# Hash products of both halves in one PSUM bank, with four small transfers, in an attention-and-MLP kernel

## The chip, the cores and the metric

The kernel runs on one core of a Trainium2 chip. The metric is device time in microseconds (us) of one execution. The median of three runs of the kernel before is 780.22 us (779.61 to 780.36).

A core has TensorE (PE, matmuls into PSUM), VectorE (DVE), ScalarE (ACT) and GpSimd (POOL); SyncE (SP) issues most transfers, ScalarE a few. Each works through its own instructions in order and waits where data isn't there.

## What is computed

Attention over 2 x 8 heads of 768 rows and 64 columns, in which a query sees only keys of the same hash bucket, then two MLPs. Cut to what matters:

```
q_bits = einsum(q, proj) > 0 ; k_bits = einsum(k, proj) > 0      # proj: 64 x 6, so six bits a row
mask   = q_bucket == k_bucket
scores = where(mask, 0.125 * q @ k.T, -1e9)
attn   = exp(scores - max) / sum ; x = attn @ v                  # per head; x becomes 1536 x 512
xn     = x / sqrt(mean(x*x) + 1e-6) * rms_g
y      = (silu(xn @ w_gate) * (xn @ w_val)) @ w_out              # 512 -> 1536 -> 512
out    = relu(y @ w_in)**2 @ w_out2                              # 512 -> 2048 -> 512
```

## The kernel before

**Tiles.** Each of 16 heads has six tiles of 128 query rows, 96 in all (`plan_slot`). For a tile TensorE makes scores S of 128x768 (`st_S`, line 626) from two sets of operands: q1 with k1 (128 rows: the value's rounded part and its rest) and q2 with k2 (76 rows). Rows 64 to 75 of q2 and k2 are the hash bits, scaled by plus or minus 2^17, so that a pair of unlike buckets gets a huge negative score: the mask comes out of the matmul itself. VectorE copies S to SBUF and takes the row's extreme value on the way (`st_min`, 637), ScalarE takes the exponential (655). Then the probabilities are split into two 16-bit parts and transposed. In tiles of kind "x" TensorE transposes (674) into one of three PSUM banks `mo`, ScalarE casts (Tx, 375) and VectorE subtracts (384). In tiles of kind "a" ScalarE casts (hla), GpSimd subtracts (384), and a transfer on SP transposes (667). Then the product with V (700) into O; after a head's last tile VectorE makes the reciprocal of the sums (708, 715) and O is scaled into `xall`, by ScalarE in six pieces (722) or by VectorE in one instruction (727).

**The hash of a head** (`hash_pe`, 494): eight matmuls of 128x384 (507) into a whole score tile S, which is 2 x 384 columns in two banks and comes from the same ring as scores. Rows 64 to 75 hold the query's bits, 96 to 107 the key's. `hash_bits` (516) thresholds rows 64 to 107, both halves at once, straight into q2; `hash_dma` (524) moves the key's rows 96 to 107 of q2 to rows 64 to 75 of k2, one transfer of 12x768. Head 0 has its own short way (532 to 545).

**The norm and the MLPs.** When a batch of eight heads is done, `plan_norm` squares xall (939, ScalarE), takes the root, scales, transposes on TensorE (982) and splits into a high part `x_hi` (990, ScalarE) and a low part `x_lo` (388, VectorE). The products (1121, 1233, 1244) use weights that are made on the way: a weight of 64-bit words is loaded, ScalarE takes an absolute value (1065), VectorE does four steps (1071, 1076, 1081, 1085), and then it is split in two (375 or 379; 384). The first batch's products run beside the second batch's attention.

**The order.** Nothing is written out by hand. `Plan` is a list scheduler that runs when the program is built: every operation has a cost for each engine that may do it, needs and buffers, and a rank; at each step the operation that can start first goes next, and ties go by rank. Ranks are constants by kind of work (`R_HASH`, `R_HDMA`, `R_X`) plus a shift per operation out of the packed table `SHIFTS`. A pair such as `D=(0.47, H_E)` is a cost and a delay that make an engine less welcome. `W0` and `W1` set how many idle matmuls (454) fill gaps at the start.

Of the kernel before, what the change touches and what calls it, by code (L numbers as in the profile page):

```python
# [12 lines left out]
F32 = mybir.dt.float32  # L13
F32R = mybir.dt.float32r
# [11 lines left out]
RQ, RK = 64, 96  # L26
NH = RK + 2 * NB
# [75 lines left out]
H_E = 2.0  # L103
# [9 lines left out]
    'c-rk(XLMFYx88eBdEb|WmIwrpA`um731A>dM>>cCQuKoa5RsyRPw666Kro;nQl+RADFGo!wNW(`gFr;86d{0+kn+CgoS'  # L113
    'E7Cp1Z#L=dSPmxa<D8e|Tn{bJm%ev(8@g?AgyVspfdh679?%v_aEx1$HKjp1~AM5G$~jS)K@{;R$@xSP5OI1|2|?7W<>'
    '0;nVn|$fWf&hHA>4@*ZTmZDqRqGxftxULn*_+pvjD!#Q3%BMy&Kf)URaXpYw7=r}EN$LJlfR1T1b#1whl+vv97-*k0dO'
    '}FCOI+=F3sro&=g$nhTd{K4LeQCFssfO#BZk|&}x4?!6a6m6s4f#{uk>1fidXrSKbd<yST!@WjMfqK%0cB8S-JJJgeZ8'
    '1(aVyBc4)hDBF=9s?jqUI?+Nd_spAe&SRCVrzuaeEPtZzjHh}JWuP)(o=XHlkF&bhiR&Zc~8G^F{n6ZnSl8$1JN@kL#q'
    'T59G3+Kjug1<b=;6c4Qef8kE=3$+z?@Oqvqt`=^=w!D?M_>s592$iR7-PSs8%`wv;B0qL&f`SS9Hd>eq)ePW7Zw}N!Ee'
    '^T!aWOv+rHyjNRX_UQ#mAH=7jR9uX$|(q(E|CDH-PFzX2J?Q$i+NJ&k`+ghxfJUCQ2AC9^<=|f}ijKC`*T=A?~S)dJyH'
    '|eqr-ncutQ~cOVzq`@D>$lQM_DqjV1ARcJ$F@K0_HzhMt9(k*l}1mQ9*lNyt$n|Mr|w|B!#IuD(&MR0;TfG=|ec|(`u>'  # L120
    'ogWWg(xvWv<)VOj=)%b0+zT)7on=r(OB)(=Z^FYb$}wL7QMq;osQ%h7w}{6GtS}V`ejaVkNEsIbW3ufI-_s6rQiXbr7w'
    'BCo6p0=H{K#PIe@F(G|`Cn&=~G4D{-7Ch1>WfouT*L7lq(tN;Q|kPU<99d+C0D{=g%=N!-F1NB4}7%%@mmJv6{`{GuL9'
# [191 lines left out]
def tile_hash_attention_moe(  # L314
# [55 lines left out]
    def f32(x):  # L370
        return x.bitcast(F32)
# [1108 lines left out]
```

## Time and profile before

| | |
|---|---|
| median of three runs | 780.22 us |
| the profiled execution | 781.11 us, its span 779.3 us |
| TensorE busy | 761.0 us, 98% of the span |
| VectorE busy | 672.7 us, 86% |
| ScalarE busy | 451.1 us, 58% |
| GpSimd busy | 230.7 us, 30% |
| mean granted TensorE clock | 0.995 |

The profile is of one execution. Busy shares are averages over stages with different limits, so the stages are read apart, from windows. The attention of the first batch fills the span up to about 139 us, the second batch's runs beside the first MLP's products up to about 304 us, and products alone follow to the end. TensorE's ends are modelled, so that a short wait can hide in its busy time. Register, semaphore and transfer-issuing instructions don't count as busy.

### The profile page before, as it was taken

To read this page: it belongs to the slowest core of one execution; us is meant where nothing else is said; L and a number is where in the kernel's file an instruction comes from. 1 tells how busy PE (TensorE), PEld (TensorE's weight loads), DVE (VectorE), ACT (ScalarE), POOL (GpSimd) and SP (SyncE) were. 2 spreads that over 40 slices of the span, in tenths; PEclk is the share of its full clock that TensorE was granted. 3 is DMA by queue.
4 is the path that set the end of the run, shared out by engine and by line. 5 is a ranking of instruction groups with operands and counts; after the bars stand their busy time and mean duration, and the time that the engine had idled before them with its cause. 6 is when DMAs were issued, how large, how long until landed. Compare 5 with 4: busy or idle time off the path is not lost.

```text
span 779.3 us, 14432 instructions
## 1 busy us (share of the span) xinstructions
PE 761.0 (98%) x5401; PEld 689.8 (89%) x5401; DVE 672.7 (86%) x1340; ACT 451.1 (58%) x898; POOL 230.7 (30%) x196
## 2 busy tenths in 40 slices
PE   8999998999999999999999999999999999999998
PEld 5788887988899999999999999988888888888886
DVE  8989899898799999999998899998579787797754
ACT  5899999868877789545543344455523243232320
POOL 6689866665676445300000000010000000000000
PEclk9999999999999999999999999999999999999999
DMA  8599875998998999423342443323111131111004
GB/s 253 129 192 184 170 161 142 162 233 191 212 176 174 190 187 202 115 108 136 135 136 81 151 147 136 118 76 131 55 55 54 55 108 54 55 55 54 28 1 162
DMA packets 127726, 100.65 MB, mean 129 GB/s; under 512 B 106548, under 2 KB 108596, under 8 KB 127656
## 3 DMA queue, kind: packets, MB, share of 16 engines
q1 hardware_dynamic: 126736, 97.34, 49.9%
q10 hardware_dynamic: 920, 2.40, 1.1%
q8 instruction: 42, 0.69, 0.4%
q14 instruction: 28, 0.23, 0.1%
HBM read 67.12 MB, written 3.15 MB: 90 GB/s over the span
## 4 chain that ended last, share of the span: by engine, by line
PE 77%; DVE 7%; ACT 6%; DMA 4%; issue 3%; POOL 2%; SPq 0%; ACTq 0%; POOLq 0%; DVEq 0%
PE mo L1121 38%; PE mo L1244 17%; PE mo L1233 12%; PE S L626 4%; PE O L700 4%; DMA Ta<-hla 3%; DVE Pa L637 1%; ACT hla L375 1%; POOL hla L384 1%; PE mo L674 1%; DVE Px L637 1%; ACT Pa L655 1%; ACT xall L722 1%; DMA wraw<-in_w 1%; ACT Px L655 1%
## 5 line engine op out<-in xcount | busy, mean ns | idle before, releaser
L1121 PE MATMUL mo<-xTA,wih 128*128 128x384 f32 (+1 forms) x512 | 138.5, 351 | 0.4 <-DVE wil L384 0.4
L1121 PE MATMUL mo<-xTD,wih 128*128 128x384 f32 (+1 forms) x512 | 136.9, 348 | 0.0
L384 POOL TENSOR_TENSOR hla<-Pa,hla 128x768 f16<-128x768 f32 x66 | 111.2, 1686 | 69.1 <-ACT hla L375 50.6
L1260 DVE TENSOR_TENSOR acc<-acc,mo 128x512 f32<-128x512 f32 (+1 forms) x164 | 100.2, 616 | 21.9 <-PE mo L1244 17.5
L1121 PEld LDWEIGHTS mo<-xTA,wih 128*128 128x128 f32 x512 | 92.9, 188 | 6.2 <-DVE wil L384 0.5
L1121 PEld LDWEIGHTS mo<-xTD,wih 128*128 128x128 f32 x512 | 93.4, 188 | 5.0
L1157 ACT ACTIVATE mt<-mo 128x512 f32<-128x512 f32 x48 | 28.7, 598 | 117.8 <-PE mo L1121 117.7
L626 PE MATMUL S<-k,q 76*128 76x384 f32 (+1 forms) x384 | 86.5, 352 | 4.5 <-DVE Pa L637 2.1
L1121 PE MATMUL mo<-xTA,wil 128*128 128x384 f32 (+1 forms) x256 | 89.4, 349 | 0.0
L1121 PE MATMUL mo<-xTD,wil 128*128 128x384 f32 (+1 forms) x256 | 89.0, 348 | 0.0
L379 POOL TENSOR_SCALAR wih<-wv 128x512 fp32r<-128x512 f32 x14 | 9.4, 668 | 265.5 <-DVE wv L1085 259.4
L626 PEld LDWEIGHTS S<-k,q 76*128 76x128 f32 (+1 forms) x384 | 64.9, 189 | 9.4 <-DVE Pa L637 4.3
L637 DVE TENSOR_SCALAR_CACHE_REDUCE Pa<-S 128x768 f32<-128x768 f32 x66 | 62.8, 952 | 7.5 <-PE S L626 7.4
L1065 ACT ACTIVATE wv<-wraw 128x512 f32<-128x512 f32 x82 | 54.5, 671 | 21.3 <-DMA wraw<-in_w 17.1
L1233 PE MATMUL mo<-yh,woh 128*128 128x384 f32 x192 | 65.3, 340 | 0.5 <-DVE wil L384 0.4
L1161 DVE TENSOR_TENSOR mu<-mt 128x512 f32<-128x512 f32 x48 | 33.3, 693 | 37.1 <-ACT mt L1157 37.0
L655 ACT ACTIVATE Pa<-Pa,b 128x768 f32<-128x768 f32 x66 | 62.2, 942 | 4.5 <-DVE b L648 1.4
L1233 PE MATMUL mo<-yh,wol 128*128 128x384 f32 x192 | 64.7, 337 | 0.0
L1233 PE MATMUL mo<-yl,woh 128*128 128x384 f32 x192 | 64.6, 337 | 0.0
L375 ACT CAST hla<-Pa 128x768 f16<-128x768 f32 x66 | 55.0, 835 | 5.5 <-DMA Ta<-hla 4.8
L1081 DVE SCALAR_TENSOR_TENSOR wv<-wraw,wv 128x512 uint32<-128x512 uint32 x82 | 56.5, 692 | 0.9
L1085 DVE SCALAR_TENSOR_TENSOR wv<-wraw,wv 128x512 uint32<-128x512 uint32 x82 | 55.7, 684 | 0.4
(152 smaller groups left out, 1815.3 us busy)
## 6 DMA issues: line engine op xcount, KB each, us to landing
wraw<-in_w SPq DMA_DIRECT2D x104, 512.0 KB, 3.8
rk<-in_k SPq DMA_DIRECT2D x12, 384.0 KB, 4.1
vr<-in_v SPq DMA_DIRECT2D x8, 384.0 KB, 4.5
out<-acc SPq DMA_DIRECT2D x12, 256.0 KB, 2.0
q<-q SPq DMA_DIRECT2D x15, 192.0 KB, 3.4
rq<-in_q SPq DMA_DIRECT2D x12, 192.0 KB, 5.0
rk<-in_k ACTq DMA_DIRECT2D x4, 384.0 KB
Ta<-hla SPq DMA_TRANSPOSE x66, 4.8
```

The lines of the kernel that those rows point to most:

```text
L375: nc.scalar.copy(out_, in_)
L384: engine[eng].tensor_tensor(out=out_, in0=in0, in1=in1, op=ALU.subtract)
L626: nc.tensor.matmul(sp[:, hf, 0:TB], d[a][0:kr, t * 128:(t + 1) * 128], d[b2][0:kr, hf * TB:(hf + 1) * TB], start=(n == 0), stop=(n == 1),)
L637: nc.vector.tensor_scalar(out=e["P"].rearrange("p (a b) -> p a b", a=2), in0=e["sp"][:, :, 0:TB], scalar1=-1e9 / SCALE, scalar2=None, op0= ...
L655: nc.scalar.activation(e["P"], e["P"], AF.Exp, bias=e["b"], scale=SCALE)
L1065: nc.scalar.activation(t, f32(wst[m]["hi"]), AF.Abs)
L1081: nc.vector.scalar_tensor_tensor(out=t, in0=hi, scalar=0xC0000000, in1=t, op0=ALU.bitwise_and, op1=ALU.bitwise_or)
L1085: nc.vector.scalar_tensor_tensor(out=t, in0=lo, scalar=29, in1=t, op0=ALU.logical_shift_right, op1=ALU.bitwise_or)
L1121: nc.tensor.matmul(ps, a[:, c * 128:(c + 1) * 128], b2[:, c, :], start=(c == 0 and n == 0), stop=(c == 3 and n == 2),)
L1233: nc.tensor.matmul(po, a[:, dc * 128:(dc + 1) * 128], b2, start=(j == 0 and n == 0), stop=(j == len(fs) - 1 and n == 2),)
L1244: nc.tensor.matmul(po, a[:, tt * 128:(tt + 1) * 128], b2, start=(j == 0 and n == 0), stop=(j == len(fs) - 1 and n == 2),)
L1260: nc.vector.tensor_tensor(out=ac, in0=ac, in1=st["p"], op=ALU.add)
```

## The change

The hash weights `wz` get 96 more columns of zeros on the left. A slice of 128 columns out of it (`hash_at`) puts the twelve bit columns at any row. The eight matmuls of a head now all add into one bank of 384 columns from the ring `mo`: the query's two halves at rows 0 and 32, the key's at 64 and 96. One threshold takes all 108 rows by 384 columns to a buffer of the ring `wv` in SBUF. Four transfers of 12x384, one a side and a half, bring the bits to q2 and k2. The scores of a head wait for all four.

Further: squares and `x_hi` of the norm may be done by VectorE as well as by ScalarE; the delay `H_E` on VectorE for the evacuation of O is 0.3, not 2.0; `SHIFTS` is a new table; `wk`, a second copy of hash weights, is gone.

```diff
-H_E = 2.0
+H_E = 0.3
 SHIFTS = (
-    'c-rk(XLMFYx88eBdEb|WmIwrpA`um731A>dM>>cCQuKoa5RsyRPw666Kro;nQl+RADFGo!wNW(`gFr;86d{0+kn+CgoS'
...
+    'c-rk(_jguBx874udsAo<n$mlaZfF;zmmsKs0sSDfP=!#1NJsz!qWIAwfk1#DT|fw2`6wa+p-Pb=f=Ou7gcOpzZ{E|U+_'
...
+    wz = ap.tile([128, 2, 2, RW + 128], F32R, name="wz")
-        nc.vector.tensor_copy(wk[:, :, RQ:RQ + 2 * NB], f32(wz[:, 1, :, RK:RK + 2 * NB]))
...
+    def hash_at(c, n, row):
+        return wz[:, c, n, RW - row:RW - row + 128]
+
     def hash_pe(eng, h):
 
         d = heads[h]
-        hp = d["hp"] = scores(s_ring(h * QT + h))
+        hp = d["hp"] = mo()[:, 0:TB]
         parts = [
-            (wz[:, 0, 0], d["q1"]), (wz[:, 0, 1], d["q1"]),
-            (wz[:, 1, 0], d["k1"]), (wz[:, 1, 1], d["k2"]),
+            (c, n, x, hf) for c, n, x in ((0, 0, "q1"), (0, 1, "q1"), (1, 0, "k1"), (1, 1, "k2"))
+            for hf in range(2)
         ]
-        for n, (a, b2) in enumerate(parts):
-            for hf in range(2):
-                nc.tensor.matmul(
-                    hp[:, hf, 0:TB], a, b2[:, hf * TB:hf * TB + TB],
-                    start=(n == 0), stop=(n == 3),
-                )
+        for j, (c, n, x, hf) in enumerate(parts):
+            nc.tensor.matmul(
+                hp, hash_at(c, n, BITS["qk"[c]][hf]), d[x][:, hf * TB:hf * TB + TB],
+                start=(j == 0), stop=(j == len(parts) - 1),
+            )
 
     def hash_bits(eng, h):
 
+        hb = heads[h]["hb"] = junk()[:, 0:TB]
         nc.vector.tensor_scalar(
-            out=heads[h]["q2"][RQ:NH, :].rearrange("p (a b) -> p a b", a=2),
-            in0=heads[h]["hp"][RQ:NH, :, 0:TB],
-            scalar1=thr[RQ:NH, 0:1], scalar2=thr[RQ:NH, 1:2], op0=ALU.is_gt, op1=ALU.mult,
-        )
-
-    def hash_dma(eng, h):
-        d = heads[h]
+            out=hb[0:NH], in0=heads[h]["hp"][0:NH], scalar1=thb[0:NH, 0:1],
+            scalar2=thb[0:NH, 1:2], op0=ALU.is_gt, op1=ALU.mult,
+        )
+
+    def hash_dma(eng, h, side, hf):
+        d, row = heads[h], BITS[side][hf]
         engine[eng].dma_start(
-            out=f32(d["k2"][RQ:RQ + 2 * NB, :]), in_=f32(d["q2"][RK:RK + 2 * NB, :])
+            out=f32(d[side + "2"][rows, hf * TB:hf * TB + TB]), in_=d["hb"][row:row + 2 * NB]
         )
...
-                r=["wz", ("ql", h, 0), ("k2", h, 0)], new=[(s_ring(h * QT + h), b)],
+                r=["wz", ("ql", h, 0), ("k2", h, 0)], new=[("mo", b)],
...
     def squares(eng, t):
-        nc.scalar.activation(junk(), xall[:, t, :], AF.Square, accum_out=ss[:, t:t + 1])
+        x = xall[:, t, :]
+        if eng == "A":
+            nc.scalar.activation(junk(), x, AF.Square, accum_out=ss[:, t:t + 1])
+        else:
+            nc.vector.scalar_tensor_tensor(
+                out=junk(), in0=x, scalar=1.0, in1=x, op0=ALU.mult, op1=ALU.mult,
+                accum_out=ss[:, t:t + 1],
+            )
...
     def x_hi(eng, st, blk, c):
...
-        nc.scalar.activation(xT[1, blk][0][:, c, :], st["p"], AF.Copy, scale=gT[:, c:c + 1])
+        xh, g = xT[1, blk][0][:, c, :], gT[:, c:c + 1]
+        if eng == "A":
+            nc.scalar.activation(xh, st["p"], AF.Copy, scale=g)
+        else:
+            nc.vector.tensor_scalar(out=xh, in0=st["p"], scalar1=g, scalar2=None, op0=ALU.mult)
```

What the new table and costs make of the order stands below as the built programs list it; a name with a number is one buffer, and rows of the changed kernel have its own line numbers.

TensorE, the hash of head 2. Before, between the sixth tile of scores of head 0 and a transpose:

```order
L626 MATMUL S<-k_167,q_177 128x384 x2
L626 MATMUL S<-k_173,q_179 128x384 x2
L507 MATMUL S<-q_351,wz 128x384 x4
L507 MATMUL S<-k_325,wz 128x384 x2
L507 MATMUL S<-k_366,wz 128x384 x2
L674 MATMUL mo<-ident,Px 128x128 x3
```

Now, inside head 1's tiles of scores:

```order
L627 MATMUL S<-k_189,q_196 128x384 x2
L627 MATMUL S<-k_202,q_210 128x384 x2
L510 MATMUL mo<-q_338,wz 128x384 x4
L510 MATMUL mo<-k_315,wz 128x384 x2
L510 MATMUL mo<-k_416,wz 128x384 x2
L627 MATMUL S<-k_189,q_196 128x384 x2
L627 MATMUL S<-k_202,q_210 128x384 x2
L627 MATMUL S<-k_189,q_196 128x384 x2
L627 MATMUL S<-k_202,q_210 128x384 x2
```

The hash of head 2 has moved behind two tiles of head 1, and it writes to `mo`, so that tiles of scores stand on both sides of it.

SP, in the first batch's attention. Before (the transfer 12x768 is the bits of heads 4 and 5, 667 the transposes of the probabilities):

```order
L465 DMA rk<-in_k 128x768
L524 DMA k_735<-q_738 12x768
L468 DMA rq<-in_q 64x768 x2
L667 DMA_TRANSPOSE Ta<-hla 128x12x128 x2
L1052 DMA wraw<-in_w 128x512
L667 DMA_TRANSPOSE Ta<-hla 128x12x128
L551 DMA vr<-in_v 128x2x384
L524 DMA k_912<-q_921 12x768
L667 DMA_TRANSPOSE Ta<-hla 128x12x128
```

Now (12x384 out of `wv` are the bits of heads 3 and 4):

```order
L668 DMA_TRANSPOSE Ta<-hla 128x12x128
L525 DMA k_484<-wv 12x384 x2
L492 DMA q_949<-q_908 64x768
L525 DMA q_442<-wv 12x384 x2
L668 DMA_TRANSPOSE Ta<-hla 128x12x128
L466 DMA rk<-in_k 128x768
L668 DMA_TRANSPOSE Ta<-hla 128x12x128
L525 DMA q_641<-wv 12x384 x2
L525 DMA k_588<-wv 12x384 x2
L1070 DMA wraw<-in_w 128x512
L668 DMA_TRANSPOSE Ta<-hla 128x12x128
```

Where one transfer stood between transposes, four stand now, in one or two pairs.

VectorE, the end of head 3. Before (708 and 715 make the sums' reciprocal, and ScalarE's order has the six copies of line 722):

```order
L516 TENSOR_SCALAR q_1360<-S,cst 44x768
L708 TENSOR_SCALAR sum<-O,sc 128x6
L384 TENSOR_TENSOR Tx<-mo,Tx 128x384
L715 RECIPROCAL sum<-sum 128x6
L637 TENSOR_SCALAR Px,m<-S 128x768
```

Now:

```order
L709 TENSOR_SCALAR sum<-O,sc 128x6
L579 TENSOR_SCALAR mo<-mo 128x2
L716 RECIPROCAL sum<-sum 128x6
L584 TENSOR_SCALAR ma<-mo 128x2
L638 TENSOR_SCALAR Px,m<-S 128x768
L728 TENSOR_TENSOR xall<-O,sum 128x6x64
```

VectorE scales O itself, behind one row minimum. Five whole heads are done so, where it was one.

## Rows read from the trace of the kernel before

**Rows 1.** Windows: start:end us, then length, busy us and count of each engine

```profile
0.00:27.00 27.00, 24.48 (x161) 16.44 (x162) 22.76 (x56) 16.09 (x30) 18.62 (x24) 1.00 0.83 234
27.00:139.00 112.00, 104.14 (x1310) 94.08 (x1309) 102.07 (x239) 108.93 (x249) 86.40 (x69) 0.98 0.79 162
139.00:220.00 81.00, 76.92 (x678) 71.89 (x676) 69.67 (x137) 61.53 (x122) 50.67 (x38) 0.98 0.98 197
220.00:304.00 84.00, 83.96 (x798) 81.88 (x798) 81.15 (x162) 68.35 (x135) 48.59 (x34) 1.00 0.98 193
304.00:376.00 72.00, 71.98 (x513) 71.30 (x511) 69.91 (x152) 41.13 (x85) 11.18 (x13) 1.00 0.42 127
```

**Rows 2.** Groups of the whole trace: busy us, mean ns of one, idle before

```profile
L516 DVE TENSOR_SCALAR q<-S,cst 44x768 fp32r<-44x768 f32 x15 | 16.3, 1086 | 3.0 <-PE S L507 2.6
L541 DVE TENSOR_SCALAR k<-mo,cst 12x384 fp32r<-12x384 f32 x2 | 1.3, 671 | 0.0
L727 DVE TENSOR_TENSOR xall<-O,sum 128x384 f32<-128x384 f32 x1 | 0.6, 558 | 0.0
L388 DVE SCALAR_TENSOR_TENSOR xTA<-mo,cst,xTA 128x384 fp32r<-128x384 f32 x8 | 4.6, 613 | 0.4 <-ACT xTA L990 0.3
L990 ACT ACTIVATE xTA<-mo,cst 128x384 fp32r<-128x384 f32 x8 | 4.2, 604 | 0.0
L384 DVE TENSOR_TENSOR q<-rq,q 64x768 fp32r<-64x768 f32 (+1 forms) x3 | 3.2, 1054 | 0.1
L1081 DVE SCALAR_TENSOR_TENSOR wv<-wraw,wv 128x512 uint32<-128x512 uint32 x82 | 56.5, 692 | 0.9
```

**Rows 3.** Groups of ScalarE between 27 and 139 us, same columns

```profile
L722 ACT ACTIVATE xall<-O,sum 128x64 f32<-128x64 f32 x42 | 9.5, 327 | 0.3
L939 ACT ACTIVATE wv<-xall 128x512 f32<-128x512 f32 x6 | 3.8, 636 | 0.0
```

**Rows 4.** Waits of VectorE, 27 to 139 us: total, times, longest

```profile
DVE Tx L384 <- ACT Tx L375: 3.9, 5, 1.6
DVE Pa L637 <- PE S L626: 2.5, 5, 0.7
```

**Rows 5.** Waits of VectorE, 139 to 220 us

```profile
DVE mu L1146 <- ACT mt L1135: 4.0, 3, 1.6
DVE Pa L637 <- PE S L626: 3.0, 3, 1.2
DVE q L516 <- PE S L507: 2.0, 1, 2.0
```

**Rows 6.** Waits of TensorE in the whole trace, same columns

```profile
PE O L700 <- DMA Ta<-hla: 4.4, 6, 1.0
PE S L626 <- DVE q L516: 1.6, 2, 1.3
```

**Rows 7.** Issues on the SP queue: start us, us taken; last two: median us to landing

```profile
64.58 0.82 SPq L524 DMA_DIRECT2D k<-q  x1
65.98 1.47 SPq L667 DMA_TRANSPOSE Ta<-hla  x1
...
out<-acc SPq DMA_DIRECT2D x12, 256.0 KB, 2.0
q<-q SPq DMA_DIRECT2D x15, 192.0 KB, 3.4
```

**Rows 8.** Pieces of the chain that ended last: start us, us, what

```profile
42.60 1.42 PE S L626 x8
105.34 0.98 PE mo L674 x9
120.22 1.11 PE O L700 x36
```

**Rows 9.** Timelines of GpSimd and VectorE at the start, same columns

```profile
1.95 1.09 POOL L1380 MEMSET ones<- 128x1188 f16 x1
...
3.32 0.17 DVE L445 TENSOR_SCALAR wz<-pjh 128x6 fp32r<-128x6 f32 x1
```

More of the change, by code (lines that the diff above doesn't have):

```diff
@@ L25 @@
 NB = 6
-RQ, RK = 64, 96
-NH = RK + 2 * NB
+RQ, RW = 64, 96
+BITS = {"q": (0, 32), "k": (64, 96)}
+NH = 96 + 2 * NB
 DM = 512
@@ L118 @@
[L118 to L122, printed above, removed]
@@ L352, in tile_hash_attention_moe @@
     every = const.tile([128, 128], F32, name="every")
-    cst = const.tile([128, 4 + NB + 4], F32, name="cst")
-    gT, pj, thr, thk = cst[:, 0:4], cst[:, 4:4 + NB], cst[:, 4 + NB:6 + NB], cst[:, 6 + NB:]
+    cst = const.tile([128, 4 + NB + 6], F32, name="cst")
+    gT, pj = cst[:, 0:4], cst[:, 4:4 + NB]
+    thr, thk, thb = (cst[:, 4 + NB + 2 * n:6 + NB + 2 * n] for n in range(3))
     warm = const.tile([128, 1], F32, name="warm")
@@ L428, in zeros @@
         engine[eng].memset(f32(wz), 0.0)
-        engine[eng].memset(f32(wk), 0.0)
     def project(eng):
@@ L796, in plan_prep @@
                 lambda e: hash_pe(e, h), s0 + R_HASH, T=1.39, use=[("k1", h)],
-                r=["wz", ("ql", h, 0), ("k2", h, 0)], new=[(s_ring(h * QT + h), b)],
+                r=["wz", ("ql", h, 0), ("k2", h, 0)], new=[("mo", b)],
             )
             add(
-                lambda e: hash_bits(e, h), s0 + R_HASH, D=1.117, r=["more"] * (s_ring(h * QT + h) == "Sb"), use=[b, ("q2", h)], w=[("bits", h)],
-            )
-            add(
-                lambda e: hash_dma(e, h), s0 + R_HDMA, r=[("bits", h)],
-                use=[("k2", h), ("q2", h)], w=[("head", h)], **dma(0.15, 0.82, 0.84),
-            )
+                lambda e: hash_bits(e, h), s0 + R_HASH, D=0.585, use=[b],
+                new=[("wv", ("hb", h))], w=[("bits", h)],
+            )
+            for side in "kq":
+                for hf in range(2):
+                    add(
+                        lambda e, side=side, hf=hf: hash_dma(e, h, side, hf), s0 + R_HDMA + 0.1 * hf,
+                        r=[("bits", h)], use=[(side + "2", h), ("hb", h)],
+                        w=[("bit", h, side, hf)], **dma(0.15, 0.5, 0.5),
+                    )
+            ready = [("bit", h, side, hf) for side in "kq" for hf in range(2)]
+            add(lambda e: None, s0 + R_HDMA, r=ready, w=[("head", h)])
     def plan_v(h):
@@ L1028, in plan_norm @@
                 use=[b] + [("xT", 1, pair)] * (not first),
-                new=[("xT" + tag, ("xT", 1, pair))] * first, A=0.464,
+                new=[("xT" + tag, ("xT", 1, pair))] * first, A=0.464, D=(0.53, 0.6),
                 w=[("xh", 1, blk, c)] + [("xt", pair)] * first,
@@ L1443, in rows @@
         return w.reshape(-1, 128, 512)
-    bound = np.zeros((128, 4), np.float32)
-    bound[RQ + NB:RQ + 2 * NB, 0] = bound[RK:RK + NB, 0] = -np.finfo(np.float32).tiny
-    bound[RQ:RQ + 2 * NB, 1] = BIG
-    bound[RK:RK + 2 * NB, 1] = -BIG
-    bound[RQ:RQ + 2 * NB, 2:4] = bound[RK:RK + 2 * NB, 0:2]
+    low = -np.finfo(np.float32).tiny
+    bound = np.zeros((128, 6), np.float32)
+    bound[RQ + NB:RQ + 2 * NB, 0] = bound[RQ:RQ + NB, 2] = low
+    bound[RQ:RQ + 2 * NB, 1], bound[RQ:RQ + 2 * NB, 3] = BIG, -BIG
+    for hf in range(2):
+        a, b = BITS["q"][hf], BITS["k"][hf]
+        bound[a + NB:a + 2 * NB, 4] = bound[b:b + NB, 4] = low
+        bound[a:a + 2 * NB, 5], bound[b:b + 2 * NB, 5] = BIG, -BIG
     host = {
```

109 lines of the change are left out of this document (57 added, 52 removed).

## The prediction

> **What bounds the kernel now.** I read the windows by stage first, then the groups, then the waits of the two fullest engines, then the SP queue. In the windows look at which engine has no room. From 220 us on TensorE is full, 83.96 of 84 us and 71.98 of 72 [rows 1], and it stays so up to the last few us. From there it only works off matmuls, and the change leaves their number alone (the orders list as many of each kind, the 37 fillers included; the hash has eight of 128x384 per head in both). So the end moves only by time that TensorE loses before 220 us: 2.5 us up to 27, 7.9 from 27 to 139, 4.1 from 139 to 220 [rows 1], and what its pipelining hides in "busy".
>
> Second, VectorE. From 27 to 376 us it is idle 9.9 + 11.3 + 2.9 + 2.1 = 26.2 us, most of it before 220 [rows 1]. From 304 to 376 it works 69.91 of 72 us while TensorE works all of them [rows 1]: it splits the weights that the products eat, just in time. I added up, by the durations of the trace, what stands on VectorE ahead of each weight's split and on TensorE ahead of its first product: between the 36th and the 45th weight the split ends within about 1 us of its use. So there TensorE cannot be early unless VectorE is too. **The gain is what VectorE's waits lose up to 376 us, less what is added to its work.**
>
> Third, who makes VectorE wait. From 27 to 139 us ScalarE works 108.93 of 112 us, fuller than any other [rows 1]; its cast of the transposed tile costs VectorE 3.9 us, late scores 2.5 [rows 4]. From 139 to 220 VectorE waits 4.0 for the gate's tanh, 3.0 for scores and 2.0 for hash products [rows 5]; the hash's waits are 2.6 in all [rows 2].
>
> **The change part by part.**
>
> *Bits.* One threshold over 44x768 takes 1.086 us, one over 12x384 0.671 [rows 2]; the 0.415 between them goes with the 384 columns rather than with partitions, so I price 108x384 at 0.67 (bounds 0.67 and 1.09). 15 x 0.415 = 6.2 us less on VectorE. The scores' ring no longer gives a place to the hash: VectorE's 2.6 us [rows 2] and TensorE's 1.6 (scores behind L516) [rows 6] have no cause left. The products now take one of three banks that the transposes use; such a wait is not in this trace: 0 to 0.67 per head, the time of the threshold, and I take 0, since three banks turn faster than two score tiles.
>
> *Transfers.* Four in place of one, 45 issues more: 50 on SP and 10 on ScalarE's queue, where it was 14 and 1. One of 12x768 holds SP 0.82 us [rows 7]; one of 12x384 between half of that and all. A head then holds SP 1.6 to 3.3 us, not 0.8. Queued behind are the transposes of the probabilities (1.47 us an issue) [rows 7], and behind those the products with V. The scores of a head now wait for the query's bits too. From the hash's end to landed bits: 0.67, four issues of at most 0.82, a landing of 2.0 to 3.4 [rows 7], or 5.9 to 7.4 us; one transpose between makes it 8.8. TensorE's own work between a head's hash and its first scores (0.71 us a tile of scores, 0.33 for three transposes, 0.56 for a tile's product with V [rows 8]) is by the order 6.7, 6.7 and 7.1 us for heads 1, 2 and 8, 8.9 for head 3, 10 or more for the others; before it was 8 to 18 in that half. So three heads may come late, by 0 to 2.1 us each; I take 0, since ScalarE and VectorE pace that half and stretch these leads, and keep 6 us as the far end.
>
> The rows show landings of 2.0 to 3.4 us and issues 0.8 apart [rows 7], so that landings overlap. The Trainium skill ("DMA: Bandwidth & Descriptors", Bandwidth) speaks against such a change: transfers under 64 KB, as these of 18, are dominated by their descriptors, and batching is the rule. By the rows four cost 2.5 us more issue than one at most, and the sum stays; by the rule, paid one after the other, it becomes the fourth rival below.
>
> *Evacuation and norm.* Up to the 55th exponential ScalarE's order has 21 scaled copies of O fewer (42 cost 9.5 us [rows 3]: 4.7), six norm casts fewer (8 cost 4.2 [rows 2]: 3.2), two squares fewer (6 cost 3.8 [rows 3]: 1.3) and, net, some casts of V, k and weights (about 2): 11 us off 109. VectorE takes, over the whole kernel, four whole evacuations at 0.56 and two halves (0.28 to 0.56), two squares at 0.69 (by L1081), three norm casts at 0.61, and three subtractions at 1.05 that GpSimd did [rows 2]; 0.75 goes. 2.9 + 1.4 + 1.8 + 3.2 - 0.75 = 8.6 us, less 6.2: **2.4 us more work**. Four of the norm's sets of transposes stand behind the 55th tile of scores on TensorE, not ahead; they cost the same.
>
> *Start.* GpSimd now clears the hash weights after the ones, whose 1.09 us [rows 9] delays this to about 2.6 us into the span; VectorE first writes them at 3.32 [rows 9], held by the constants: nothing.
>
> *Sum.* From 27 to 139: ScalarE's claim falls to 98 us, VectorE's stays near 102. VectorE's best stretch, 220 to 304, ran at 81.15 of 84 [rows 1], 97%: 102 / 0.97 = 105.5, or, rounded up, 4.5 us of waits for 9.9 (bounds 0 and 9.9). From 139 to 220 I take off the hash's 2.0 and 0.5 of the rest: 8.8 for 11.3 (bounds 5 and 14). After that, unchanged. Waits fall by 7.9, work grows by 2.4. Last, by the same adding up, the tightest weight's split stands 1.2 us later against its product in the new order than in the old. 7.9 - 2.4 - 1.2 = 4.3 us. The profiled execution, 781.1 us with a span of 779.3, would come to 776.8; it lay 0.9 above the median of 780.2, so the median comes to 775.9.
>
> **Rivals.**
>
> *Given back.* VectorE's order has 92 weight steps ahead of the 96th row minimum where it had 108: 16 steps of up to 0.69 us [rows 2] move from the attention into 304 to 376 us, which has 2.1 us free [rows 1]. If the new order makes waits of its own in the attention, so that only the hash's 2.6 us goes: 2.6 - 2.4 - 1.2 = -1.0, so 780 to 781. For it: two engines near 100% wait for each other more than one does. Against: ScalarE's 11 us would have to be worth nothing.
>
> *Slower: transposes behind the bits.* SP runs in order, and a set of four waits there for its threshold, with transposes behind it. TensorE already waits for six transposes, 4.4 us in all [rows 6]; at those places the queue has no slack, and three more issues of 0.8 make each 2.4 us later. At two of them (4.8 us) the gain is gone. I price three, 7.2 us: 775.9 + 7.2 = 783. Against: the 59 issues between 27 and 139 us, such as those in [rows 7], hold SP some 60 of 112 us, so it has room on average.
>
> *More.* If VectorE's waits for ScalarE go wholly (3.9 [rows 4] and the tanh's 4.0 [rows 5]), the hash's 2.6 and 2.5 of the scores', waits fall by 13: 13 - 2.4 - 1.2 = 9.4, so 771. The stages before 220 would then run as 220 to 304 does.
>
> *Transfers one after the other.* If each of the four lands before the next is sent, at 0.41 and 2.0 us [rows 7], bits take 0.67 + 4 x 2.41 = 10.3 us: heads 1, 2, 3, 7 and 8 are late by 3.6, 3.6, 1.4, 0.2 and 3.2, 12 us in all: 788. [...] Issues 0.8 apart speak against it.
>
> *Not what it says.* If 108 partitions read from PSUM cost the old 1.09 us, VectorE gets 6.2 us more: 782. The two threshold rows speak against it.
>
> **How the numbers follow.** Forecast 775.9: 0.48, its own range 773 to 778.5. More, 771: 0.17. Given back, 780.5: 0.15. Transposes behind the bits, 783: 0.13. Transfers one after the other, 788: 0.03. Not what it says, 782: 0.04. The range 769.5 to 783 leaves out a tenth on either side. Faster by over 0.2% (below 778.7; about what a measurement of this kernel can tell from no change) 0.65, same 0.15, slower 0.20.
>
> **What would show it.** Right: ScalarE's busy share from 27 us to the first product falls below 95% and VectorE's rises above it; the 108x384 threshold takes 0.65 to 0.7 us; the waits behind L516 are gone; TensorE is full some 4 us earlier than 220. Wrong: products with V wait for transposes more than 4.4 us in all, or scores for the bits' transfers (the two rivals of SP); TensorE waits for weight splits between 290 and 380 us (given back). An idle TensorE that loses its clock would add to either: its mean is 0.98 in both stretches before 220 [rows 1], and I assume as much after.

## The result and the profile after

The changed kernel takes 784.38 us (median of 17 runs, 780.98 to 786.56), the kernel before on the same chip 778.06 (17 runs): ratio 1.0070, interval 1.0055 to 1.0085. By this ratio it is slower by 5.5 us (the two medians stand 6.3 apart), where 4.3 less was forecast. The profiled spans, 784.7 and 779.3, stand 5.4 apart; the changed kernel's profiled execution is the slowest of its 17.

Windows of the changed kernel (start:end, length, busy us of PE, PEld, DVE, ACT, POOL, granted clock, DMA share, GB/s), beside [rows 1]:

```profile
27.00:139.00 112.00, 99.12 (x1284) 91.04 (x1283) 101.15 (x237) 96.50 (x210) 79.68 (x66) 0.97 0.81 165
139.00:220.00 81.00, 75.06 (x703) 71.96 (x703) 71.51 (x134) 65.25 (x131) 56.27 (x39) 0.96 0.91 190
220.00:304.00 84.00, 84.00 (x846) 81.74 (x845) 79.25 (x167) 70.76 (x138) 46.62 (x30) 1.00 0.91 197
304.00:376.00 72.00, 72.00 (x452) 71.07 (x451) 71.50 (x150) 39.46 (x77) 5.93 (x7) 1.00 0.36 126
```

ScalarE fell from 108.93 to 96.50 of 112 us, as forecast (98). VectorE did not fill up: from 27 to 376 us it is idle 10.85 + 9.49 + 4.75 + 0.50 = 25.6 us, where it was 26.2. TensorE lost 12.9 us from 27 to 139 (before: 7.9), 5.9 from 139 to 220 (4.1), and nothing from there to 376.

Groups of VectorE (busy us, mean ns, idle before): the threshold on 108 rows, the scaling of O, a square, the norm's cast.

```profile
L518 DVE TENSOR_SCALAR wv<-mo,cst 108x384 f32<-108x384 f32 x15 | 10.1, 672 | 0.0
L728 DVE TENSOR_TENSOR xall<-O,sum 128x384 f32<-128x384 f32 (+1 forms) x7 | 3.5, 496 | 0.1
L950 DVE SCALAR_TENSOR_TENSOR wv<-xall 128x512 f32<-128x512 f32 x2 | 2.9, 1430 | 0.7 <-DMA q<-wv 0.7
L1008 DVE TENSOR_SCALAR xTA<-mo,cst 128x384 fp32r<-128x384 f32 x3 | 1.7, 603 | 0.0
```

The threshold takes 0.672 us where it took 1.086 [rows 2], and nothing waits ahead of it. What TensorE waits for now (total, times, longest), beside [rows 6]:

```profile
PE S L627 <- DVE Pa L638: 5.9, 5, 3.1
PE O L701 <- DMA Ta<-hla: 4.8, 4, 1.3
PE O L701 <- DVE Tx L388: 4.2, 2, 4.0
```

Two long waits are new (4.0 and 3.1 us; before, the longest was 1.3), and the granted clock falls behind each (0.97 and 0.96 for the two stages, 0.98 in both before). The first, at 126 us: VectorE's queue, then SP's (start, us taken; x2 is two issues in one row).

```profile
124.87 0.55 DVE L388 TENSOR_TENSOR Tx<-mo,Tx 128x384 f16<-128x384 f32 x1
125.34 0.15 DVE L970 TENSOR_TENSOR rt<-rr 128x3 f32<-128x3 f32 x1
128.11 0.55 DVE L565 TENSOR_REDUCE mx<-vr 128x1 f32<-128x384 f32 x1 [2.62 <-DMA vr<-in_v]
128.58 1.44 DVE L972 TENSOR_TENSOR rt<-rt,ss 128x3 f32<-128x3 f32 x1
129.94 0.55 DVE L388 TENSOR_TENSOR Tx<-mo,Tx 128x384 f16<-128x384 f32 x1
```
```profile
117.65 2.25 SPq L469 DMA_DIRECT2D rq<-in_q  x2
119.99 0.80 SPq L525 DMA_DIRECT2D q<-wv  x1
120.89 0.78 SPq L525 DMA_DIRECT2D k<-wv  x1
121.73 0.71 SPq L525 DMA_DIRECT2D q<-wv  x1
122.54 0.46 SPq L552 DMA_DIRECT2D vr<-in_v  x1
```

VectorE stands at the maximum of V and waits 2.62 us for a load that SP issued behind three sets of bits. The 128x3 step behind it takes 1.44 us, where the others of its line take 0.15 (more on this under "Evacuation and norm"). The split of the transposed tile that comes next is what TensorE needs. The second wait, at 180 us, in ScalarE's rows:

```profile
175.40 0.66 ACT L1083 ACTIVATE wv<-wraw 128x512 f32<-128x512 f32 x1 [1.40 <-DMA wraw<-in_w]
175.40 1.52 ACTq L525 DMA_DIRECT2D k<-wv  x2
176.97 1.94 ACTq L525 DMA_DIRECT2D q<-wv  x2
178.95 0.63 ACT L1083 ACTIVATE mo<-wraw 128x512 f32<-128x512 f32 x1 [2.89 <-DMA q<-wv]
```

VectorE waits 3.0 us for the first absolute value here, which itself waited for its weight's load. Then ScalarE issues four sets of bits one behind the other, from 175.40 to 178.91 us, and only then makes the second value. (The row puts these 2.89 us down to `q<-wv`, but the four issues fill them.) VectorE works off the late weight steps, and the row minimum that TensorE needs comes last.

### The profile page after: what moved, and what is told of

Read it like the earlier page. It is cut to its first block, busy times and chain, and to the rows that moved or that the text cites. A ratio compares the mean times of both kernels' runs of the same rounds, so it can differ in the third digit from the quotient of the medians.

```text
span 784.7 us, 14459 instructions
## 1 busy us (share of the span) xinstructions
PE 758.8 (97%) x5401; PEld 691.1 (88%) x5401; DVE 678.1 (86%) x1353; ACT 449.1 (57%) x872; POOL 223.4 (28%) x183
## 4 chain that ended last, share of the span: by engine, by line
PE 75%; DVE 8%; DMA 6%; ACT 4%; POOL 3%; issue 2%; ACTq 0%; SPq 0%; POOLq 0%; DVEq 0%
PE mo L1139 36%; PE mo L1262 17%; PE mo L1251 11%; PE S L627 5%; PE O L701 4%; DMA Ta<-hla 3%; DMA wraw<-in_w 2%; POOL hla L388 2%; DVE Pa L638 1%; PE mo L510 1%; PE mo L675 1%; DVE wv L1103 1%; DVE wv L1099 1%; ACT Px L656 1%; DVE Px L638 1%
## 5 line engine op out<-in xcount | busy, mean ns | idle before, releaser
L388 POOL TENSOR_TENSOR hla<-Pa,hla 128x768 f16<-128x768 f32 x65 | 109.6, 1692 | 55.1 <-ACT hla L379 50.8
L1278 DVE TENSOR_TENSOR acc<-acc,mo 128x512 f32<-128x512 f32 (+1 forms) x164 | 100.6, 617 | 21.7 <-PE mo L1262 17.5
L627 PEld LDWEIGHTS S<-k,q 76*128 76x128 f32 (+1 forms) x384 | 66.7, 193 | 10.1 <-DVE Pa L638 7.1
L383 POOL TENSOR_SCALAR wih<-wv 128x512 fp32r<-128x512 f32 x12 | 7.5, 625 | 230.8 <-DVE wv L1103 219.4
L1103 DVE SCALAR_TENSOR_TENSOR wv<-wraw,wv 128x512 uint32<-128x512 uint32 x82 | 57.4, 701 | 0.5
L1099 DVE SCALAR_TENSOR_TENSOR wv<-wraw,wv 128x512 uint32<-128x512 uint32 x82 | 56.9, 696 | 0.8
```

The lines of the kernel that those rows point to most:

```text
L388: engine[eng].tensor_tensor(out=out_, in0=in0, in1=in1, op=ALU.subtract)
L627: nc.tensor.matmul(sp[:, hf, 0:TB], d[a][0:kr, t * 128:(t + 1) * 128], d[b2][0:kr, hf * TB:(hf + 1) * TB], start=(n == 0), stop=(n == 1),)
L1099: nc.vector.scalar_tensor_tensor(out=t, in0=hi, scalar=0xC0000000, in1=t, op0=ALU.bitwise_and, op1=ALU.bitwise_or)
L1103: nc.vector.scalar_tensor_tensor(out=t, in0=lo, scalar=29, in1=t, op0=ALU.logical_shift_right, op1=ALU.bitwise_or)
L1278: nc.vector.tensor_tensor(out=ac, in0=ac, in1=st["p"], op=ALU.add)
```

## The experiments

Two theories stood against each other. **Transfers:** the four issues per head hold the queues and delay what stands behind. **Order:** the new order places VectorE's in-order waits badly, whatever is transferred. Ratios are to the kernel before on the same chip; "against changed" is (ratio - 1.0070) x 779 us. The last three columns are from the profiled execution, against the kernel before: its span, VectorE's busy time in the whole trace, VectorE's idle time from 27 to 376 us. A profiled execution lies up to 3.2 us from the median of its kernel (e12 above, e15 below), so these columns don't decide on a few us; the ratios do.

| run | ratio, interval | against changed | span | VectorE work | VectorE idle |
|---|---|---|---|---|---|
| changed | 1.0070, 1.0055 to 1.0085 | | +5.4 | +5.4 | -0.6 |
| e1 four, old order | 1.0257, 1.0226 to 1.0288 | +14.6 | +17.4 | +0.5 | +15.9 |
| e2 old hash, new order | 1.0298, 1.0269 to 1.0326 | +17.8 | +23.5 | +15.7 | +7.5 |
| e3 bits twice | 1.0471, 1.0443 to 1.0500 | +31.2 | +38.6 | +4.7 | +33.4 |
| e4 V before bits | 1.0047, 1.0032 to 1.0062 | -1.8 | +3.2 | +4.4 | -1.5 |
| e5 three transfers | 0.9998, 0.9984 to 1.0011 | -5.6 | -2.2 | +7.0 | -8.8 |
| e6 no key bits | 0.9937, 0.9915 to 0.9959 | -10.4 | -7.0 | +2.9 | -9.9 |
| e7 VectorE's order | 1.0076, 1.0050 to 1.0102 | +0.5 | +2.8 | +5.6 | -2.5 |
| e8 ScalarE's to SP | 1.0071, 1.0044 to 1.0098 | +0.1 | +4.0 | +4.2 | 0.0 |
| e9 key on ScalarE | 1.0021, 0.9998 to 1.0043 | -3.8 | +1.7 | +5.9 | -5.5 |
| e10 key on GpSimd | 1.0166, 1.0141 to 1.0191 | +7.5 | +10.8 | +12.5 | -2.1 |
| e11 norm, evacuation back | 1.0129, 1.0104 to 1.0154 | +4.6 | +6.4 | -0.7 | +6.8 |
| e12 three, V first | 1.0015, 0.9998 to 1.0032 | -4.3 | +2.3 | +8.0 | -5.6 |
| e13 key at a quarter | 1.0044, 1.0015 to 1.0073 | -2.0 | +5.0 | +5.3 | -1.0 |
| e14 one transfer | 1.0114, 1.0072 to 1.0157 | +3.4 | +8.8 | +15.6 | -6.9 |
| e15 three, one on ScalarE | 0.9998, 0.9972 to 1.0025 | -5.6 | -4.4 | +7.7 | -11.1 |
| e16 evacuation back | 1.0115, 1.0065 to 1.0164 | +3.5 | +8.2 | +2.0 | +5.8 |
| e17 three, two on ScalarE | 1.0016, 0.9996 to 1.0036 | -4.2 | -2.1 | +7.2 | -9.2 |

In every row the span follows the sum of the last two columns to 1.3 us or better. An engine's work and idle time always add up to the span; what the rows show is that VectorE's idle time before 27 and after 376 us hardly changes, so that the last two columns say where a variant's time went. They don't say why.

e6 and e13 leave bits of the key out: they price transfers and are no kernels to use. In e2 to e17 the order stays the one that was planned for the changed kernel, up to the moves that are named.

### Adding transfers: e1 and e3

```diff
 # e1: the kernel before
-        engine[eng].dma_start(
-            out=f32(d["k2"][RQ:RQ + 2 * NB, :]), in_=f32(d["q2"][RK:RK + 2 * NB, :])
-        )
+        for r0 in (RQ, RQ + 2 * NB):
+            for c in (slice(0, TB), slice(TB, S)):
+                engine[eng].dma_start(
+                    out=f32(d["k2"][r0:r0 + 2 * NB, c]), in_=f32(d["q2"][RK:RK + 2 * NB, c])
+                )
 # e3: the changed kernel
+        for r0 in (RQ, RQ + 2 * NB):
+            engine[eng].dma_start(
+                out=f32(d[side + "2"][r0:r0 + 2 * NB, hf * TB:hf * TB + TB]),
+                in_=d["hb"][row:row + 2 * NB],
+            )
```

> The kernel before, in its own order, with four transfers of 12x384 per head where it issues one of 12x768 (the key bits in two halves to their rows, and the same two halves again to twelve rows that nothing reads). Nothing else differs. Transfers (the theory that the extra issues, 0.71 to 0.97 us each in the changed kernel, hold the queue and delay what stands behind them): 45 more issues hold SP about 34 us more, and the time rises by 3 to 8 us, ratio 1.004 to 1.010. Order (the rival: the new order of VectorE and of the weight loads makes the two long stalls by itself, and the transfers lie beside other work): within 1 us, ratio 0.999 to 1.0015.

> The changed kernel with each of its 12x384 transfers issued twice, the second time to twelve rows that nothing reads: eight per head for four, 60 issues more. Transfers: if the first 45 cost about 5 us, 60 more cost at least as much, since the queue is fuller: 6 to 12 us more than the changed kernel, ratio to before 1.015 to 1.022. Order: 0 to 1.5 us more, ratio 1.007 to 1.009.

45 more transfers cost the old order 20 us (0.44 each), 60 more cost the new one 31 (0.52 each): far from what the order theory gave, and two to three times what the transfer theory gave at most. TensorE's waits in e1 say where, beside [rows 6] (transposes 4.4 in all):

```profile
PE O L702 <- DMA Ta<-hla: 10.6, 12, 2.2
PE mo L574 <- DVE mx L566: 5.3, 3, 2.6
```

Twelve waits for transposes where there were six, and 5.3 us for maxima of V, whose loads come late. The order can't be blamed: e1 has the old one. SP's issues that start from 27 to 139 us hold its queue, added up one by one, 59.7 us (59 issues) in the kernel before, 76.0 (78) in e1, 86.1 (84) in the changed kernel, 89.6 (97) in e3.

### Taking transfers away: e5, e6, e13

```diff
 # e5: products at rows 64, 76, 88, 100; the threshold writes into the query's operand
-BITS = {"q": (0, 32), "k": (64, 96)}
+BITS = {"q": (64, 76), "k": (88, 100)}
-        hb = heads[h]["hb"] = junk()[:, 0:TB]
+        hb = heads[h]["hb"] = heads[h]["q2"][:, 0:TB]
-            out=hb[0:NH], in0=heads[h]["hp"][0:NH], scalar1=thb[0:NH, 0:1],
+            out=hb[RQ:NH], in0=heads[h]["hp"][RQ:NH], scalar1=thb[RQ:NH, 0:1],
 # and no transfer of ("q", 0); e6 instead: no transfer of ("k", 0), ("k", 1)
 # e13: the key's transfers at a quarter of their width
+            out=f32(d[side + "2"][rows, hf * TB:hf * TB + (TB if side == "q" else TB // 4)]),
```

> The changed kernel, in its order, with three transfers per head for four: the threshold (48x384, rows 64 to 112) writes into the query's operand, where the bits of the query's first half are in place at once; the other three sets go by transfers as they do now. 15 issues fewer. Transfers, at the 0.45 to 0.52 us per issue that the two runs with more transfers gave: 6.7 to 7.8 us less than the changed kernel, ratio to before 0.997 to 0.998. If only the issues at the two long stalls matter: 0 to 2 us less, 1.004 to 1.007. The threshold itself should take 0.67 us on 48 rows as on 108.

> The changed kernel without the two transfers per head that bring the key's bits (left out: the scores are then computed with key rows that hold no bits); 30 issues fewer, two per head left, order as it is. Transfers: 13 to 16 us less than the changed kernel if each issue costs what it cost when they were added, ratio to before 0.986 to 0.990; less if VectorE's work sets a floor, which by its 25.6 us of idle time up to 376 us it does not before 8 us. Order: 0 to 2 us less, 1.004 to 1.007.

> The changed kernel with the key's transfers at 12x96 for 12x384 (left out: three quarters of the key's bits never arrive): four issues per head as now, 4.6 KB for 18 in two of them. If the price goes with the number of issues: within 2 us of the changed kernel, ratio to before 1.005 to 1.009, and the issue of a quarter holds the queue 0.7 to 0.8 us as now. If it goes with the bytes: three quarters of the 10.4 us that leaving these transfers out gave, ratio 0.996 to 0.999, and the issue holds the queue 0.2 to 0.4 us.

15 fewer give back 5.6 us (0.37 each), 30 fewer 10.4 (0.35 each): less than the 6.7 to 7.8 and 13 to 16 that the price of added transfers had let expect, and far above the 0 to 2 of the other side. e5's windows:

```profile
27.00:139.00 112.00, 103.72 (x1309) 93.74 (x1308) 105.24 (x243) 99.19 (x214) 83.05 (x68) 0.96 0.82 168
139.00:220.00 81.00, 78.36 (x742) 75.09 (x740) 75.24 (x144) 69.20 (x139) 56.78 (x40) 1.00 0.92 201
```

VectorE is at 105.24 and 75.24; its idle time falls by 8.8 us against the kernel before (forecast: 7.9). TensorE waits for transposes 1.0 us in all. One thing besides the count differs in e5: the threshold's output no longer sits in the ring `wv` that the weight steps share. That the transfers hold this ring until they land shows in the changed kernel as VectorE's 0.7 us ahead of a square (L950 above), put down to `q<-wv`, and in e4 below. How much of e5's gain is the ring's, no run shows.

e13 asks whether bytes or issues count. Its rows of line 525 (minimum, median and maximum ns; `k` is 12x96, `q` 12x384):

```profile
L525 SPq DMA_DIRECT2D q<-wv x26: 713/744/1352, 20.3 to 243.7; - x26
L525 SPq DMA_DIRECT2D k<-wv x24: 714/764/886, 18.0 to 242.0; - x24
```

A quarter of the bytes holds the queue as long. The time is 2.0 us below the changed kernel's, which the intervals don't tell from nothing (they overlap), and its own interval, from 1.0015 up, leaves out the 0.996 to 0.999 of the bytes: **the price goes with the number of transfers, not with their bytes**. The Trainium skill ("DMA: Bandwidth & Descriptors", Bandwidth) says that transfers under 64 KB are dominated by their descriptors; its figures there are for loads that GpSimd issues. e13 agrees in so far as cutting bytes shows no gain, and its rows put the issuing side at 0.74 to 0.76 us a transfer.

### Which queue: e4, e8, e9, e10, e12, e15, e17

The edits name the engine that issues at the same place of the program, or move one load; "three" is e5's kernel.

```diff
 # e4, e12, e15: V of heads 12 and 13
+        ahead(find("load_v", h=12)[0], find("load_k", h=11)[0])          # e4
+        ahead(find("load_v", h=12)[0], find("hash_dma", h=9, side="q", hf=1)[0])  # e12, e15
 # e8
+        for o in find("hash_dma"):
+            o.eng = "S"
 # e9, e17: "A"; e10: "P"; e15: "A" for hf=1 alone
+        for o in find("hash_dma", side="k"):
+            o.eng = "A"
```

> The changed kernel with one instruction moved: the load of V for heads 12 and 13 goes ahead of the three transfers of bits that stand before it on SP (issued 119.99 to 122.44 us; the load at 122.54 landed at about 128.1, where VectorE had waited 2.62 us for it and TensorE 4.1 us for VectorE). Transfers: the load lands about 2.5 us earlier, VectorE's wait there ends, the stall at 126 us shrinks from 4.1 to about 1.5 us, and the time falls by 1.5 to 3 us, ratio to before 1.003 to 1.005. Order: something else ends late in its place, and the time falls by less than 1 us.

> The changed kernel with the ten transfers of bits that ScalarE issues (each 0.7 to 1.0 us of its queue, four in a row at 175 us, where ScalarE then stood idle 2.89 us) issued by SP at the same places of the program. Transfers on ScalarE's queue: the stall at 180 us shrinks by about 1 us and ScalarE gets 8 to 9 us back in 11 to 220 us: 1 to 3 us less than the changed kernel, ratio 1.003 to 1.006. Transfers on SP's queue (the rival): SP, which issues the transposes too, is the fuller one, and the time rises by 1 to 4 us, ratio 1.008 to 1.012.

> The changed kernel with the 30 transfers of the key's bits all issued by ScalarE, at the same places of the program; the number of transfers is as it was. By the traces SP's instructions hold its queue 84.9 of 112 us from 27 to 139 in the changed kernel, 61.5 in the kernel before, 72.6 in the one without the key's bits. If the price is SP's queue (what stands behind an issue there waits): about 22 issues of 0.8 us leave SP, ScalarE (96.5 of 112 us busy) takes them beside its work: 3 to 8 us less than the changed kernel, ratio to before 0.997 to 1.003. If the price is that of the transfers themselves (their landings, their places among those under way at once), or if ScalarE's own queue is as tight: within 2 us, 1.005 to 1.010, or more.

> The same, with the 30 transfers of the key's bits issued by GpSimd. GpSimd works 80 of 112 us from 27 to 139, on the second parts of the casts, which feed the transposes. If the price is SP's queue and an issue on GpSimd costs no more than on SP (0.8 us): 3 to 8 us less than the changed kernel, 0.997 to 1.003. If GpSimd's issues take longer, or delay the casts behind them: 2 to 10 us more, 1.010 to 1.020.

> Three transfers per head (as in the run with three) and the load of V for heads 12 and 13 ahead of the bits (as in the run that moved it). The one took 5 to 6 us off the changed kernel, the other 2. If both act on the same queue at different places they add up: 7 to 8 us less than the changed kernel, ratio to before 0.996 to 0.999. If the first already freed what the second moves: as with three, 0.999 to 1.001.

> Three transfers per head, V ahead of the bits, and the transfer of the key's second half issued by ScalarE: at most two per head on SP. Thirty of the key's on ScalarE took about 3.8 us off the changed kernel; fifteen here: 1 to 3 us less than with three on SP, ratio to before 0.996 to 0.999. If three per head already fit in SP's queue: no change, 0.999 to 1.002.

> Three transfers per head, the two of the key issued by ScalarE, the one of the query by SP; nothing else moved. SP then issues as many transfers of bits as in the kernel before (15). If the price is SP's queue alone: 3 to 6 us less than with three on SP, ratio to before 0.992 to 0.996. If ScalarE's queue takes over the price, or the waits that are left are of another kind: 0.997 to 1.003.

e4, in which the load also passes the four loads ahead of the bits, takes 1.8 us off (the intervals overlap a little). In it the wait moved:

```profile
DVE wv L518 <- DMA k<-wv: 1.9, 1, 1.9
```

The load now lands in time, and three instructions later the next head's threshold waits 1.9 us for a place in the ring, which an earlier head's bits still hold: a second cost of the transfers, that of waiting for their landing.

e9 puts 30 of the 60 on ScalarE: -3.8 us, with SP's queue held 73.5 of 112 us. So SP's queue is part of the price, since the number of transfers stayed; about a third of what leaving the same 30 out gave. e8, the other way with ten, changes nothing, which neither side had expected: ScalarE's 2.89 us are gone there, but its wait for the weight's load ahead of them is 2.97 us where it was 1.40. e10 costs 7.5 us though an issue takes GpSimd only 0.56 us (x30, busy 16.8). GpSimd works in order too, and waits for thresholds with the casts behind it, as in the row below. VectorE's busy time grew by 7.1 us with the same instructions: single ones ran long beside GpSimd's ("Evacuation and norm").

```profile
63.01 0.54 POOL L525 DMA_DIRECT2D k<-wv  x1 [2.94 <-DVE wv L518]
```

With three per head (e12, e15, e17) neither the earlier load nor a change of queue gives more; the three intervals and e5's overlap. In e17 SP's queue is held 61.4 us, hardly more than in the kernel before (59.7), and the time is no better than e5's: ScalarE's queue takes the price over, or what is left of it is of another kind. No variant with all bits in place is shown to be faster than the kernel before; e5 and e15 equal it (0.9998).

### The order and the other parts: e7, e2, e11, e16, e14

```diff
 # e7: VectorE's order at the two long waits
+        for o in find("st_S", i=63) + find("st_min", i=63):
+            ahead(o, find("w_f32", m=(1, 2, 1, 0), n=0)[0])
+        for n in range(2):
+            ahead(find("bound_v", h=12, n=n)[0], find("pool")[0])
 # e2: products, threshold and transfer as in the kernel before
-        hp = d["hp"] = mo()[:, 0:TB]
+        hp = d["hp"] = scores(s_ring(h * QT + h))
 # e11 (e16: st_evac alone)
+        for o in find("st_evac") + find("squares") + find("x_hi"):
+            o.eng = "A"
 # e14: a bank and a threshold per half, one transfer
+        nc.vector.tensor_scalar(
+            out=heads[h]["q2"][RQ:NH, hf * TB:hf * TB + TB], in0=heads[h]["hp", hf][RQ:NH],
...
```

> The changed kernel with VectorE's order alone changed at the two long stalls: the two maxima of V for heads 12 and 13 stand just ahead of the matmul that needs them, behind the splits of the transposed tiles; and the row minimum behind which TensorE waited 3.3 us at 180 us stands ahead of four weight steps, a split and a gate product. Every transfer stays where it is. Order: both stalls shrink, by 2 to 4 and by 2 to 2.7 us, and the half clock behind them goes: 4 to 6 us less than the changed kernel, ratio to before 0.999 to 1.002. Transfers: what waited for the load waits a little later, 0 to 2 us less, 1.004 to 1.007.

> The changed kernel in its own order and with its own choice of engines, but with the hash of before: products into a tile of the scores' ring, one threshold over 44x768, one transfer of 12x768 at the place of the first of the four. Transfers: the 45 issues are gone, VectorE gets 6.2 us more work (15 x 0.415): the stalls of 4.1 and 3.3 us at 126 and 180 us shrink to 1 to 2 us each, and the time falls by 1 to 5 us against the changed kernel, ratio to before 1.000 to 1.005. Order: the stalls stay, VectorE's 6.2 us are added, and the time rises by 2 to 6 us, ratio to before 1.010 to 1.015.

> The changed kernel with the evacuations, squares and norm casts that its planner gave to VectorE back on ScalarE, at the same places of the program: the six evacuations, two squares and three norm casts, about 6 us less on VectorE (which waits 25.6 us up to 376) and about 8 us more on ScalarE, most of it between 27 and 160 us. If VectorE sets the pace (the prediction's way): 2 to 5 us less, 1.001 to 1.005. If the transfers do (this study's): within 2 us, 1.004 to 1.010.

> The changed kernel with the six evacuations that VectorE does (four whole, two halves) back on ScalarE; squares and norm casts stay as in the changed kernel. Back on ScalarE evacuations, squares and casts cost 4.6 us. If it was the evacuations: 3 to 5 us more than the changed kernel, ratio 1.010 to 1.014. If the norm: within 1 us, 1.006 to 1.009.

> The changed kernel, its order and its choice of engines, with one transfer of 12x768 per head as before the change, issued by SP at the place of the first of the four. For that the two halves' products go into two banks in turn, and two thresholds over 44x384 (0.67 us each) write into the query's operand. 45 issues fewer, 15 thresholds of 0.67 us more on VectorE. Price per issue of 0.35 us (from the runs with 15 and 30 fewer): 45 x 0.35 = 16 us less; VectorE's 10 us more, of which its idle time hides some: 6 to 12 us less than the changed kernel, ratio to before 0.992 to 0.999. If VectorE's work counts in full and more, since the transposes' banks are now held longer: as the changed kernel or slower, 1.004 to 1.012.

e7 refutes the order theory in its form: both long waits are gone from the trace (the transposed tile's 4.0 us is 0.2, the scores' 3.1 at most 1.3), and the time did not move (+0.5). Others came in their place. VectorE's longest wait and two of TensorE's in e7:

```profile
DVE wv L1089 <- ACT wv L1083: 4.5, 1, 4.5
PE O L701 <- DMA Ta<-hla: 6.8, 7, 1.6
PE mo L1251 <- DVE mu L1164: 3.1, 1, 3.1
```

What VectorE does first, it pays for at the next thing that is late: the weight's absolute value still waits for its load.

e2 missed both expectations. 6.2 us of its 17.8 is the dearer threshold; much of the rest shows as TensorE's waits for the ring of scores:

```profile
PE S L629 <- DVE q L519: 12.9, 13, 1.8
PE S L512 <- DVE Pa L640: 7.8, 8, 1.4
```

So in an order that was planned without the hash in that ring, putting it back costs much more than the 2.6 and 1.6 us that the old order's rows showed [rows 2, 6]; what an order planned anew would make of it, no run shows.

e11 and e16: the seven evacuations on VectorE (five whole, two halves; one was there before) back on ScalarE cost 3.5 us, with the norm 4.6. VectorE's work falls by 6.1 us in e11 and its waits grow by 7.4: ScalarE's relief pays for VectorE's work and a little more. In e11 TensorE waits for ScalarE's scaling of O, 0.2 us in the changed kernel:

```profile
PE O L701 <- ACT xall L723: 4.5, 5, 2.1
```

The expectation of the prediction's way (2 to 5 us less) is refuted, and the other (within 2 us) is missed too.

e14 is the dearest lesson. 45 issues fewer (SP's queue held 57.8 us, transposes waited for 0.6 us), and still 3.4 us slower than the changed kernel. The second threshold adds 10.2 us to VectorE, its waits fall by 6.3 only, and new ones come:

```profile
PE mo L511 <- DVE Tx L389: 3.5, 7, 0.8
PE mo L674 <- DVE q L517: 2.3, 2, 1.1
```

Products wait for a bank that a transposed tile still holds, and transposes for one that a threshold holds: the wait that the prediction bounded at 0 to 0.67 per head, and which one set of products per head doesn't show.

## Why the prediction was wrong

**What bounds: right as to the place.** TensorE is full from 220 us on (84.00 and 72.00 us), and loses 7.5 us more than before up to there, for 5.4 of span. That VectorE paces it, and not only goes with it, the table can't show: e11 took 6.1 us of work off VectorE and the time grew.

**Bits: right.** 0.672 us on 108 rows (0.67 taken), also 0.686 on 48 in e5; the waits behind the old threshold are gone, and by e2 this was worth more, in this order, than was counted.

**Transfers: the step that failed.** "I take 0, since ScalarE and VectorE pace that half", with 6 us as the far end. Measured as the price of a change in their number, a transfer is worth 0.35 to 0.52 us of the time; 45 at the lower end of that make 16 us. That is an estimate: no run has the cheap threshold with one transfer. The issue itself was within its bounds (0.41 to 0.82), at the upper end: 0.74 and 0.77 (medians of the query's and the key's on SP), since halving the columns bought almost nothing against 0.81 for 12x768 (the text allowed half). The kernel's planner, too, reckons 0.5 us (`dma(0.15, 0.5, 0.5)` in `plan_prep`); whether an order planned with 0.75 would lose less, no run shows. What was wrong is the reading of "SP has room on average". Only three heads' scores were looked at as those who could come late for the bits; scores wait for bits nowhere in the changed kernel. Those who came late stood behind the bits: transposes (e1), V's load (the wait at 126 us), a weight's load (e8), and, through the ring `wv`, squares (0.7 us in the changed kernel) and thresholds (1.9 in e4).

**The rival "transposes behind the bits"** (783, chance 0.13) named the mechanism, but its place was too narrow; that its time nearly came is luck, since it priced 7.2 us for three transposes where the transfers cost some 16 and other terms gave a part back. In the changed kernel TensorE waits 4.8 us for transposes, hardly more than the 4.4 before: the forecast's own sign of this rival came, but by 0.4 us. V's load paid there instead. In e1 transposes cost 10.6.

**"Transfers one after the other"** (788): the issues stand 0.8 us apart as before, not a landing apart (119.99, 120.89 and 121.73 us in the rows above). That the price goes with the number was right; that transfers wait for each other was not.

**Evacuation and norm:** VectorE's work grew by 5.4 us, not 2.4. The operations that came and went are those of the forecast; what it lacks is that single ones ran long. Measured against the shortest of the same operation, shape and buffers in any run, 16 of VectorE's instructions in the changed kernel took over 0.25 us longer, 10.1 us in all; in the kernel before 12, 5.4 in all; in e10 22, 17.5 in all. Each of them, in every trace, overlaps an instruction of GpSimd, which is busy 28% of the changed kernel's span. One of the two squares took 0.69 us, as forecast; the other:

```profile
135.61 2.18 DVE L950 SCALAR_TENSOR_TENSOR wv<-xall 128x512 f32<-128x512 f32 x1 [0.72 <-DMA q<-wv]
135.60 1.64 POOL L388 TENSOR_TENSOR hla<-Pa,hla 128x768 f16<-128x768 f32 x1
```

The 1.44 us of the 128x3 step at 128.58 us lie beside such a subtraction too. That GpSimd is the cause is argued from this, and no edit tests it. That the evacuation pays all the same is shown by e11 and e16.

**Waits:** 7.9 us less was forecast and 0.6 came. With three transfers it is 8.8 (e5), with two 9.9 (e6). The gain was there and the transfers ate it. That 8.8 is close to 7.9 is in part luck: 102 / 0.97 is 105.2, which leaves 3.2 us of waits from 27 to 139, and the text rounded this up to 4.5; e5 has 6.8 there, and 5.8 from 139 to 220 where 8.8 was forecast. The 0.98 that the text assumed for the clock came out as 0.97 and 0.96, behind the two long waits. That the sum then is 7.9 - 2.4 - 1.2 and not more is not borne out either way: no run has the cheap threshold with one transfer, since one instruction can't put both halves' bits where they belong.

**Open:** how the price of a transfer splits between the queue that it holds (e9: about a third, for the key's 30) and the landing that the ring and later instructions wait for. e5 changes both at once.

## What to carry to other kernels

A queue that is half free on average is not free: before an issue is added to an in-order queue, look at what stands behind it at each place, loads for later stages too, and at the buffers that stay held until it lands. One small transfer split into four holds the queue nearly four times as long (0.74 us each against 0.81), since the time goes with their number; look for an output that is in place at once, as e5's query half is, before adding one. The longest wait in a trace (e7) is where lateness surfaces, not where it arises: add up work and waits of the fullest engine, look at what moved between the two, and let the measured time judge the edit.

## What was not expected of the hardware

- An issue of a 12x96 transfer between SBUF rows holds SP's queue 0.764 us (median of 24), one of 12x384 0.744 (26; both in e13), one of 12x768 0.807 (14; kernel before). The load of V, 384 KB from memory, held it 0.46 us (median of 8, changed kernel).
- VectorE's square over 128x512 took 0.69 us once and 2.18 us once, a 128x3 step 0.15 and 1.44: the long ones lay beside a subtraction of GpSimd, and every instruction of VectorE that ran over 0.25 us long in these traces overlapped one of GpSimd's (16 in the changed kernel).
